# Reordering the first 15 microseconds of a matmul-bound kernel: two normalizations to ScalarE, tiles 0 and 1 by products, weight pieces in half-K groups

## The chip, the cores and the metric

One core of a Trainium2 chip. Kernels are compared only within the same rounds. The time is that of one execution on the device, in microseconds (us). One profiled execution is called "one look", and an execution is called slow here when it took over 621.5 us, a limit that was chosen after the first times were seen.

## The reference

An input x of 2048 rows by 1024 columns is layer-normalized per row. Two branches use the result: a dense layer with a Mish activation (`w1`: 1024x3584, `w2`: 3584x1024) and a diagonal state-space layer (projection by B, a complex scan over 2048 steps, projection by C). Their sum and x make the output.

```python
xn = _layernorm(x, axis=-1)
return x + _A_ref(xn, Lambda, B, C, log_dt, Dskip) + _B_ref(xn, w1, b1, w2)
# _B_ref:  h = xn @ w1 + b1;  act = h * tanh(softplus(h));  return act @ w2
```

## The kernel before

The rows go in four blocks of 512, and a block is four tiles (0 to 3) of 128 rows. Each block runs 28 weight tiles of `w1` (called f), the projection by B, the scan, and the output products. Only the **head**, the first 15 us of block 0, is changed.

To start TensorE before the layer norm is ready, the head multiplies the first seven weight tiles by *raw* x of tiles 0 and 1 (`first_raw`), and corrects mean and scale afterwards on VectorE and GpSimd (`raw_scale`, `raw_add`, with rows spread by `first_spread`). Tiles 2 and 3 are normalized first, transposed on TensorE, and multiplied by the same seven weight tiles (`first_rest`: 56 matmuls of 256 columns, the **milestone** of all that follows). Filler matmuls keep TensorE busy while the first data arrive (from 1.04 us on). Each engine ran its own list in the order of the program (VectorE's statistics of tile 2 start at 8.46 us, after the normalization of 8.00 that stands ahead of them); the helper classes put in the semaphore waits.

```python
# order of emission in the head (cut)
keep_busy(18); first_transpose(0); keep_busy(14); first_transpose(1); keep_busy(6)
for q in range(2):                       # ScalarE: turn tiles 0, 1 out of PSUM, roots
    first_copy(q, AC, 0, 4); first_copy(q, AC, 4, NK)
    first_sums_v(q, 0); first_sums_v(q, 1); first_var_v(q); first_sqrt(q)
first_scale(0); first_apply(0); first_scale(1); first_split(); first_apply(1)   # VectorE
for q in range(2):
    transpose_dma(q)                     # sync queue: DMA transposes of normalized tiles 0, 1
for i in range(4, NRING):
    ring_load()                          # sync queue: weight pieces 5 to 7 (1 to 4 went earlier)
...
for f in range(4): first_raw(f, 0, NK // 2)       # weight piece 1
first_spread()
for f in range(4): first_raw(f, NK // 2, NK)      # weight piece 2
# ... statistics and normalization of tiles 2 and 3 on VectorE ...
first_raw(4, 0, NK // 2); first_raw(5, 0, NK // 2)   # weight piece 3
first_transpose(2); first_copy(2, AC)
first_raw(4, NK // 2, NK); first_raw(5, NK // 2, NK) # weight piece 4
first_transpose(3); first_copy(3, VE)
first_raw(6)
```

`load_x(PO, 1, q)` loads the four x tiles of block 1 from GpSimd's queue after the fourth of eight tables:

```python
for j in range(NJ):
    phases(j)
    if j == 3:
        for q in range(NQ):
            load_x(PO, 1, q)
...
if f in (14, 16, 18, 20): ln_stats_only(1, (f - 14) // 2)   # VectorE
if f < 24 and f % 3 == 2: transpose_B(f // 3)               # sync queue, DMA transposes
```

Of the kernel before, what the change touches and what calls it, by code (L numbers as in the profile page):

```python
# [5 lines left out]
ALU = mybir.AluOpType  # L6
AF = mybir.ActivationFunctionType
DT = mybir.dt

P = 128  # L10
# [146 lines left out]
def build_kernel(nc, A_x, A_Lambda_re, A_Lambda_im, A_B_re, A_B_im, A_C_re, A_C_im,  # L157
                 A_log_dt, A_Dskip, B_w1, B_b1, B_w2, out):
    bf16, f32, i32 = DT.bfloat16, DT.float32, DT.int32
# [6 lines left out]
    NK = D // P  # L166
# [8 lines left out]
    PE = Queue(nc, "pe")  # L175
    VE = Queue(nc, "ve")
    AC = Queue(nc, "ac")
    PO = Queue(nc, "po")
    SP = Queue(nc, "sp")

    def sb(name, shape, dtype):
# [3 lines left out]
    NRING = 7  # L185
# [17 lines left out]
    xnT = sb("xnT", [P, NK, TB], bf16)  # L203
    b_xnT = [Buf("xnT%d" % q, parts=[Buf("xnT%d_%d" % (q, h)) for h in range(2)]) for q in range(NQ)]
# [3 lines left out]
    xx = sb("xx", [P, 2, NQ, D], bf16)  # L208
    b_xx = [[Buf("xx%d_%d" % (i, q), parts=[Buf("xx%d_%d_%d" % (i, q, h)) for h in range(2)])
             for q in range(NQ)] for i in range(2)]  # L210
    s_xx = [[DmaSem(nc, "d_xx%d_%d" % (i, q)) for q in range(NQ)] for i in range(2)]
    xn = sb("xn", [P, NQ, D], bf16)
# [38 lines left out]
    def ps16(i):  # L251
        return ps[:, i, :].bitcast(bf16)
# [28 lines left out]
    def early(name, shape, dtype, where):  # L281
        b_early.append(Buf(name))
        return nc.alloc_sbuf_tensor_at(name, shape, dtype, offset=base_c + where), b_early[-1]
# [6 lines left out]
    rr, b_rr = early("rr", [P, 4], f32, 10240)  # L290
    rh, b_rh = early("rh", [P, 4], bf16, 10272)
    rl, b_rl = early("rl", [P, 4], bf16, 10304)
    ncs, _ = early("ncs", [P, NR], f32, 10752)
    b_ncs = [Buf("ncs%d" % f) for f in range(NR)]
    b_early += b_ncs
    ra = [early("ra%d" % i, [P, 2 * P], f32, 12288 + 1024 * i) for i in range(2)]
    rb = [early("rb%d" % i, [P, 2 * P], f32, 14336 + 1024 * i) for i in range(2)]

# [8 lines left out]
    def load_x(queue, blk, q):  # L307
        r0 = blk * TB + q * P
        i = blk % 2
        queue.dma(lambda e: e.dma_start(xx[:, i, q, :], A_x[0, r0:r0 + P, :]),  # L310
                  s_xx[i][q] if blk else s_x0[q], writes=[b_xx[i][q]])
# [16 lines left out]
    def ring_load():  # L328
        i = n_loaded[0]
        if i >= len(items):  # L330
            return
        n_loaded[0] += 1
        kind, g = items[i]
        s = i % NRING
        if kind == "w1":

            dst = ring[:, s, :].rearrange("p (k f) -> p k f", k=NK // 2)
            r0 = (g % 2) * D // 2
            src = B_w1[r0:r0 + D // 2, (g // 2) * 512:(g // 2 + 1) * 512].rearrange("(k p) f -> p k f", p=P)
        else:  # L340
            dst = ring[:, s, :].rearrange("p (f d) -> p f d", f=2)
            src = B_w2[g * 256:(g + 1) * 256, :].rearrange("(f p) d -> p f d", p=P)
        SP.dma(lambda e: e.dma_start(dst, src), s_ring[s], writes=[b_ring[s]])  # L343

    for i in range(4):
        ring_load()
        if i < 2:
            load_x(SP, 0, 2 + i)


    filler = sb("filler", [P, P], bf16)
# [17 lines left out]
    def first_sums_v(q, h):  # L369
        s = q % 2  # L370
        vop(lambda e: e.bn_stats(stats[:, s, h, :], xx[:, 0, q, h * 512:(h + 1) * 512]),
            reads=[b_xx[0][q].parts[h]], writes=[b_stats[s]])

    def first_var_v(q):
        s = q % 2
        vop(lambda e: e.bn_aggr(mv[:, q, :], stats[:, s, :, :]), reads=[b_stats[s]], writes=[b_mv[q]])

    def first_sqrt(q):
        aop(lambda e: e.activation(rc(q, 1), mv[:, q, 1:2], AF.Sqrt, bias=kon[:, 2:3]),
            reads=[b_mv[q], b_kon], writes=[b_rs1[q]])  # L380

    def first_apply(q):
        vop(lambda e: e.tensor_scalar(xn[:, q, :], xx[:, 0, q, :], mv[:, q, 0:1], root(q),
                                      op0=ALU.subtract, op1=ALU.mult),
            reads=[b_xx[0][q], b_mv[q], b_rr if q < 2 else b_rs1[q]], writes=[b_xn[q]])

    def bank_T(q, k):
        if q < 2 and k >= NK // 2:
            return 4 + q
        return 6 + q % 2  # L390

    def first_transpose(q):

        for k in range(NK):
            bank, d = bank_T(q, k), slice(k * P, (k + 1) * P)
            src, b_src = (xx[:, 0, q, d], b_xx[0][q]) if q < 2 else (xn[:, q, d], b_xn[q])
            PE.mm(lambda e, bank=bank, d=d, src=src: e.transpose(ps16(bank)[:, d], src, ident[:]),  # L397
                  reads=[b_src.parts[k // (NK // 2)], b_ident], writes=[b_ps[bank]],
                  first=k == 0 or bank != bank_T(q, k - 1), last=k == NK - 1 or bank != bank_T(q, k + 1))

    def first_copy(q, queue, k0=0, k1=NK):
        dst, b_dst = (xr, b_xr[q][k0 // 4]) if q < 2 else (xnT, b_xnT[q])
        dst = dst[:, k0:k1, q * P:(q + 1) * P]
        bank = bank_T(q, k0)
        srcp = ps16(bank).rearrange("p (k t) -> p k t", k=NK)[:, k0:k1, :]
        if queue is AC:
            aop(lambda e: e.copy(dst, srcp), reads=[b_ps[bank]], writes=[b_dst])
        else:
            vop(lambda e: e.tensor_copy(dst, srcp), reads=[b_ps[bank]], writes=[b_dst])

    def root(q):
        return rr[:, q:q + 1] if q < 2 else rc(q, 1)

    def first_scale(q):

        y, b_y = root(q), b_rr if q < 2 else b_rs1[q]
        vop(lambda e: e.reciprocal(y, rc(q, 1)), reads=[b_rs1[q]], writes=[b_y])
        if q < 2:
            vop(lambda e: e.tensor_tensor(rr[:, 2 + q:3 + q], mv[:, q, 0:1], y, op=ALU.mult),
                reads=[b_mv[q], b_rr], writes=[b_rr])  # L420

    def first_split():
# [60 lines left out]
    def transpose_dma(q):  # L483
        SP.dma(lambda e: e.dma_start_transpose(xnT[:, :, q * P:(q + 1) * P], xn[:, q, :]),
               s_xnT[q], reads=[b_xn[q]], writes=[b_xnT[q]])
# [3 lines left out]
    def b1(f):  # L489
        return par[:, 3 * NJ + f:3 * NJ + f + 1]  # L490
# [13 lines left out]
    def keep_busy(n, behind=()):  # L504
        for i in range(n):
            PE.mm(lambda e: e.matmul(ps[:, 3, 0:P], lhsT=filler[:], rhs=filler[:], start=True, stop=True),
                  reads=[b_filler] + (list(behind) if i == 0 else []), writes=[b_ps[3]], first=i == 0, last=i == n - 1)

    keep_busy(18)
    first_transpose(0)  # L510
    keep_busy(14)
    first_transpose(1)
    keep_busy(6)
    aop(lambda e: e.activation(rs[:, :, 3], kon[:, 2:3].to_broadcast([P, NQ]), AF.Sqrt), reads=[b_kon], writes=b_rs)
# [5 lines left out]
        first_var_v(q)  # L520
        first_sqrt(q)
    first_scale(0)
    first_apply(0)
    first_scale(1)
    first_split()
    first_apply(1)
    for q in range(2):
        transpose_dma(q)
    for i in range(4, NRING):
        ring_load()  # L530
        if i == 5:
            SP.dma(lambda e: e.dma_start(dsk[:], A_Dskip.partition_broadcast(P)), s_dsk, writes=[b_dsk])

    def w1_tile(base, f, k):

# [4 lines left out]
    def first_raw(f, k0=0, k1=NK):  # L540

        for k in range(k0, k1):
            s, w = w1_tile(0, f, k)
            PE.mm(lambda e, k=k, w=w: e.matmul(ps[:, f, 0:2 * P + 1], lhsT=w, rhs=xr[:, k, 0:2 * P + 1],  # L544
                                               start=k == 0, stop=k == NK - 1),
                  reads=[b_ring[s], b_xr_all, b_xr[0][k // 4], b_xr[1][k // 4]], writes=[b_ps[f]],
                  first=k == 0, last=k == NK - 1)
# [8 lines left out]

    def raw_scale(f):
        (a, b_a), (b, b_b) = ra[f % 2], rb[f % 2]
        vop(lambda e: e.tensor_scalar(ncs[:, f:f + 1], ps[:, f, 2 * P:2 * P + 1], -1.0, None, op0=ALU.mult),
            reads=[b_ps[f]], writes=[b_ncs[f]])  # L560
        vop(lambda e: e.tensor_tensor(a[:], ps[:, f, 0:2 * P], yz[:, 0:2 * P], op=ALU.mult),
            reads=[b_ps[f], b_yz], writes=[b_a])
        pop(lambda e: e.tensor_scalar(b[:], yz[:, 2 * P:4 * P], ncs[:, f:f + 1], b1(f), op0=ALU.mult, op1=ALU.add),
            reads=[b_yz, b_ncs[f], b_par], writes=[b_b])

    def raw_add(f):
        (a, b_a), (b, b_b) = ra[f % 2], rb[f % 2]
# [8 lines left out]

    for f in range(4):
        first_raw(f, 0, NK // 2)
    PE.op(lambda e: e.transpose(ps16(6)[:, 0:NST], st[:, :], ident[0:NST, 0:NST]),
          reads=[b_st, b_ident], writes=[b_ps[6]])  # L580
    aop(lambda e: e.copy(par[:, :], ps16(6)[:, 0:NST]), reads=[b_ps[6]], writes=[b_par])
    first_spread()
    for f in range(4):
        first_raw(f, NK // 2, NK)
    for h in range(2):
        first_sums_v(2, h)
    first_var_v(2)
    first_sqrt(2)
    first_sums_v(3, 0)
    first_scale(2)  # L590
    first_apply(2)
    first_sums_v(3, 1)
    first_var_v(3)
    first_sqrt(3)
    first_raw(4, 0, NK // 2)
    first_raw(5, 0, NK // 2)
    first_transpose(2)
    first_copy(2, AC)
    first_raw(4, NK // 2, NK)
    first_raw(5, NK // 2, NK)  # L600
    raw_scale(0)
    first_scale(3)
    first_apply(3)
    first_transpose(3)
    raw_scale(1)
    first_copy(3, VE)
    first_raw(6)
    raw_add(0)
    for f in range(2, NR):
        raw_scale(f)  # L610
# [366 lines left out]
```

## Time and profile before

| | before |
|---|---|
| time, first three executions | 620.79, 620.87, 623.14 us |
| span of the profiled one | 619.6 us |
| TensorE busy | 616.1 us |
| first raw matmul | 7.01 us |
| milestone: start of the 56 matmuls | 15.45 us |

TensorE is the bound, and the prediction below shows the lines for it. What the change moves between engines are these groups of VectorE's timeline (start, length, line, instruction, result and source, shape, count); the two normalizations at 6.95 and 8.00 stand in the way of the statistics of tile 2 at 8.46.

```profile
6.95 0.55 DVE L383 TENSOR_SCALAR xn<-xx,mv,rr 128x1024 bf16<-128x1024 bf16 x1
...
8.00 0.55 DVE L383 TENSOR_SCALAR xn<-xx,mv,rr 128x1024 bf16<-128x1024 bf16 x1
8.46 1.41 DVE L371 BATCH_NORM_STATS2 stats<-xx 128x6 f32<-128x512 bf16 x2
...
13.00 0.55 DVE L383 TENSOR_SCALAR xn<-xx,mv,rs 128x1024 bf16<-128x1024 bf16 x1
```

### The profile page before, as it was taken

To read this page: it belongs to the slowest core of one execution; us is meant where nothing else is said; L and a number is where in the kernel's file an instruction comes from. 1 tells how busy PE (TensorE), PEld (TensorE's weight loads), DVE (VectorE), ACT (ScalarE), POOL (GpSimd) and SP (SyncE) were. 2 spreads that over 40 slices of the span, in tenths; PEclk is the share of its full clock that TensorE was granted. 3 is DMA by queue.
4 is the path that set the end of the run, shared out by engine and by line. 5 is a ranking of instruction groups with operands and counts; after the bars stand their busy time and mean duration, and the time that the engine had idled before them with its cause. 6 is when DMAs were issued, how large, how long until landed. Compare 5 with 4: busy or idle time off the path is not lost.

```text
span 619.6 us, 7424 instructions
## 1 busy us (share of the span) xinstructions
PE 616.1 (99%) x2957; PEld 288.4 (47%) x2957; DVE 467.3 (75%) x698; ACT 247.5 (40%) x161; POOL 53.1 (9%) x57
## 2 busy tenths in 40 slices
PE   9999999999999999999999999999999999999998
PEld 7644444444444444444444444444444444444444
DVE  6989999999467599998147659999624856999603
ACT  4589997441079940000009992000001999000000
POOL 2899100000100000000010000000000000000000
DMA  8999986840454401783054430286203542033001
GB/s 249 252 254 298 225 167 202 206 136 0 146 191 140 135 2 37 204 201 103 17 187 135 158 114 1 96 184 189 75 35 107 173 162 68 1 123 116 1 0 69
DMA packets 97917, 79.94 MB, mean 129 GB/s; under 512 B 51034, under 2 KB 80346, under 8 KB 97882
## 3 DMA queue, kind: packets, MB, share of 16 engines
q1 hardware_dynamic: 94384, 72.17, 42.3%
q10 hardware_dynamic: 2538, 4.14, 1.8%
q0 software_dynamic: 960, 3.15, 1.8%
q8 instruction: 24, 0.39, 0.3%
q14 instruction: 11, 0.09, 0.1%
HBM read 63.19 MB, written 4.19 MB: 109 GB/s over the span
## 4 chain that ended last, share of the span: by engine, by line
PE 98%; DMA 1%; SPq 1%; issue 0%; DVE 0%
PE ps L820 49%; PE ps L740 29%; PE ps L762 18%; DMA ring<-in_B_w_dram 1%; PE ps L553 1%; PE ps L544 0%; SPq L310 0%; PE ps L834 0%; PE ps L397 0%; SPq L343 0%; SPq L314 0%; DVE xx L888 0%
## 5 line engine op out<-in xcount | busy, mean ns | idle before, releaser
L820 PE MATMUL ps<-ring,act 128*128 128x512 bf16 x896 | 194.0, 379 | 0.0
L740 PE MATMUL ps<-xnT,ring 128*128 128x512 bf16 x840 | 182.0, 379 | 0.0
L718 ACT ACTIVATE act<-hb 128x3584 bf16<-128x3584 bf16 x16 | 50.9, 3183 | 220.6 <-DVE hb L749 220.4
L820 PEld LDWEIGHTS ps<-ring,act 128*128 128x128 bf16 x896 | 87.7, 98 | 105.7
L740 PEld LDWEIGHTS ps<-xnT,ring 128*128 128x128 bf16 x840 | 82.2, 98 | 98.9
L749 DVE TENSOR_SCALAR hb<-ps,par 128x512 bf16<-128x512 f32 (+1 forms) x112 | 80.0, 730 | 52.6 <-PE ps L740 51.7
L762 PE MATMUL ps<-xnT,BT 128*128 128x512 bf16 x512 | 111.2, 379 | 0.0
L820 PE MATMUL ps<-CT,hT 128*128 128x512 bf16 x506 | 109.9, 379 | 0.0
L767 DVE TENSOR_TENSOR mt<-ps,tab 128x1024 bf16<-128x1024 f32 x64 | 75.4, 1219 | 13.3 <-PE ps L762 11.7
L762 PEld LDWEIGHTS ps<-xnT,BT 128*128 128x128 bf16 x512 | 50.1, 98 | 60.4
L820 PEld LDWEIGHTS ps<-CT,hT 128*128 128x128 bf16 x506 | 49.5, 98 | 59.7
L785 DVE TENSOR_TENSOR_SCAN hT<-cs,qi,hT 128x512 bf16<-128x512 f32 x48 | 58.9, 1269 | 0.0
L865 DVE TENSOR_TENSOR xx<-ps,xx 128x1024 bf16<-128x1024 f32 (+1 forms) x16 | 18.8, 1190 | 45.1 <-PE ps L820 45.0
L720 ACT ACTIVATE act<-act 128x3584 bf16<-128x3584 bf16 x16 | 51.0, 3190 | 0.2
L719 ACT ACTIVATE act<-act 128x3584 bf16<-128x3584 bf16 x16 | 51.0, 3190 | 0.2
L790 DVE TENSOR_TENSOR mt<-hT,tab 128x1024 bf16<-128x1024 bf16 x64 | 41.4, 688 | 1.1
L725 DVE TENSOR_TENSOR act<-act,hb 128x3584 bf16<-128x3584 bf16 x16 | 33.2, 2075 | 2.3 <-ACT act L720 2.3
L310 POOL DMA_DIRECT2D xx<-in_A_x_dram x12 | 6.7, 560 | 249.4 <-DVE xx L865 245.1
L694 ACT ACTIVATE ct<-CT,cs 128x512 f32<-128x512 bf16 x16 | 11.5, 718 | 25.3 <-DVE CT L696 25.3
L719 ACT ACT_TABLE_LOAD x16 | 20.5, 1283 | 0.3
L720 ACT ACT_TABLE_LOAD x16 | 20.5, 1283 | 0.3
L785 DVE TENSOR_TENSOR_SCAN hT<-cs,hT 128x512 bf16<-128x512 f32 x16 | 18.7, 1208 | 0.0
(101 smaller groups left out, 294.1 us busy)
## 6 DMA issues: line engine op xcount, KB each, us to landing
ring<-in_B_w_dram SPq DMA_DIRECT2D x112, 512.0 KB, 4.0
out_dram<-xx ACTq DMA_DIRECT2D x15, 256.0 KB, 2.1
xx<-in_A_x_dram POOLq DMA_DIRECT2D x12, 256.0 KB, 4.3
xx<-in_A_x_dram SPq DMA_DIRECT2D x3, 256.0 KB, 4.4
xx<-in_A_x_dram SPq DMA_DIRECT2D x2, 128.0 KB, 2.3
dsk<-in_A_Dskip_dram SPq DMA_DIRECT2D x1, 256.0 KB, 7.4
xnT<-xn SPq DMA_TRANSPOSE x14, 4.6
BT<-in_A_B_re_dram SPq DMA_TRANSPOSE x8, 6.3
```

The costliest lines, as they stand in the source:

```text
L718: aop(lambda e: e.activation(a, hs, AF.Exp), reads=[b_hb[g % 2]], writes=[b_act[g]])
L719: aop(lambda e: e.activation(a, a, AF.Ln, bias=1.0), reads=[b_act[g]], writes=[b_act[g]])
L720: aop(lambda e: e.activation(a, a, AF.Tanh), reads=[b_act[g]], writes=[b_act[g]])
L725: vop(lambda e: e.tensor_tensor(a, a, hs, op=ALU.mult), reads=[b_act[g], b_hb[g % 2]], writes=[b_act[g]])
L740: PE.mm(lambda e, k=k, w=w: e.matmul(ps[:, bank, :], lhsT=w, rhs=xnT[:, k, :], start=k == 0, stop=k == NK - 1), reads=[b_ring[s]] + b_xnT, ...
L749: vop(lambda e: e.tensor_scalar(hb[:, hs, ts], ps[:, bank, ts], b1(f), None, op0=ALU.add), reads=[b_ps[bank], b_par], writes=[b_hbf[hs]])
L762: PE.mm(lambda e, j=j, ci=ci, k=k, bank=bank: e.matmul(ps[:, bank + ci, :], lhsT=BT[:, ci, j, k, :], rhs=xnT[:, k, :], start=k == 0, stop= ...
L767: vop(lambda e, s=s, u=u, j=j: e.tensor_tensor(mt[:, s, :, :], u, tab[:, s, j, :].unsqueeze(1).to_broadcast([P, 2, TB]), op=ALU.mult), rea ...
L785: vop(lambda e, ci=ci, init=init: e.tensor_tensor_scan(out=hT[:, ci, j, :], data0=cj("r", j).to_broadcast([P, TB]), data1=hT[:, ci, j, :], ...
L790: vop(lambda e, s=s: e.tensor_tensor(mt[:, s, :, :], hT[:, :, j, :], tab[:, s, j, :].unsqueeze(1).to_broadcast([P, 2, TB]), op=ALU.mult), ...
L820: PE.mm(lambda e: e.matmul(ps[:, u, :], lhsT=lhsT, rhs=rhs, start=st_, stop=last), reads=reads, writes=[b_ps[u]], first=st_, last=last)
L865: vop(lambda e: e.tensor_tensor(xr, src, xr, op=ALU.add), reads=b_ps[bank:bank + n] + [b_x], writes=[b_x])
```

## The change

The intent: take the two normalizations off VectorE, so that tiles 2 and 3 are ready sooner; issue five weight pieces ahead of the DMA transposes; and arrange the raw matmuls in half-K groups around the transposes of tiles 2 and 3, which now share PSUM bank 7. Tiles 0 and 1 are turned by ordinary products with the identity, whose results are fp32 and take a whole bank per half.

```diff
@@ transfers up front: one more weight piece
         if i < 2:
             load_x(SP, 0, 2 + i)
+    ring_load()
@@ normalization of tiles 0, 1 on ScalarE (bias = -mean * rstd)
     def first_apply(q):
+        if q < 2:
+            aop(lambda e: e.activation(xn[:, q, :], xx[:, 0, q, :], AF.Identity, bias=rr[:, 2 + q:3 + q], scale=root(q)),
+                reads=[b_xx[0][q], b_rr], writes=[b_xn[q]])
+            return
@@ banks, and products in place of transposes
-        if q < 2 and k >= NK // 2:
-            return 4 + q
-        return 6 + q % 2
+        if q < 2:
+            return 4 + q + 2 * (k < NK // 2)
+        return 7
 ...
+            put = (lambda e, bank=bank, o=o, src=src: e.matmul(
+                ps[:, bank, o:o + P], lhsT=src, rhs=ident[:], start=True, stop=True)) if q < 2 else (
+                lambda e, bank=bank, d=d, src=src: e.transpose(ps16(bank)[:, d], src, ident[:]))
@@ order (cut)
-    keep_busy(14)
+    keep_busy(16)
 ...
+    first_apply(1)
+    aop(lambda e: e.copy(par[:, :], ps16(4)[:, 0:NST]), reads=[b_ps[4]], writes=[b_par])
 ...
-    first_raw(4, 0, NK // 2)
-    first_raw(5, 0, NK // 2)
-    first_transpose(2)
-    first_copy(2, AC)
-    first_raw(4, NK // 2, NK)
-    first_raw(5, NK // 2, NK)
+    first_transpose(2)
+    first_copy(2, AC, 0, 4)
+    first_sqrt(3)
+    first_copy(2, AC, 4, NK)
     raw_scale(0)
+    for f in range(4, NR):
+        first_raw(f, 0, NK // 2)
     first_scale(3)
     first_apply(3)
     first_transpose(3)
     raw_scale(1)
     first_copy(3, VE)
-    first_raw(6)
+    for f in range(4, NR):
+        first_raw(f, NK // 2, NK)
+    for q in range(2):
+        transpose_dma(q)
+    for i in range(5, NRING):
+        ring_load()
```

More of the change, by code (lines that the diff above doesn't have):

```diff
@@ L292, in build_kernel @@
     rl, b_rl = early("rl", [P, 4], bf16, 10304)
-    ncs, _ = early("ncs", [P, NR], f32, 10752)
-    b_ncs = [Buf("ncs%d" % f) for f in range(NR)]
-    b_early += b_ncs
+    csum, _ = early("csum", [P, NR], f32, 10752)
+    b_csum = [Buf("csum%d" % f) for f in range(NR)]
+    b_early += b_csum
     ra = [early("ra%d" % i, [P, 2 * P], f32, 12288 + 1024 * i) for i in range(2)]
@@ L382, in first_apply @@
     def first_apply(q):
+        if q < 2:
+            aop(lambda e: e.activation(xn[:, q, :], xx[:, 0, q, :], AF.Identity, bias=rr[:, 2 + q:3 + q], scale=root(q)),
+                reads=[b_xx[0][q], b_rr], writes=[b_xn[q]])
+            return
         vop(lambda e: e.tensor_scalar(xn[:, q, :], xx[:, 0, q, :], mv[:, q, 0:1], root(q),
                                       op0=ALU.subtract, op1=ALU.mult),
-            reads=[b_xx[0][q], b_mv[q], b_rr if q < 2 else b_rs1[q]], writes=[b_xn[q]])
+            reads=[b_xx[0][q], b_mv[q], b_rs1[q]], writes=[b_xn[q]])
     def bank_T(q, k):
-        if q < 2 and k >= NK // 2:
-            return 4 + q
-        return 6 + q % 2
+        if q < 2:
+            return 4 + q + 2 * (k < NK // 2)
+        return 7
     def first_transpose(q):
@@ L396, in first_transpose @@
             src, b_src = (xx[:, 0, q, d], b_xx[0][q]) if q < 2 else (xn[:, q, d], b_xn[q])
-            PE.mm(lambda e, bank=bank, d=d, src=src: e.transpose(ps16(bank)[:, d], src, ident[:]),
-                  reads=[b_src.parts[k // (NK // 2)], b_ident], writes=[b_ps[bank]],
+            o = (k % (NK // 2)) * P
+            put = (lambda e, bank=bank, o=o, src=src: e.matmul(
+                ps[:, bank, o:o + P], lhsT=src, rhs=ident[:], start=True, stop=True)) if q < 2 else (
+                lambda e, bank=bank, d=d, src=src: e.transpose(ps16(bank)[:, d], src, ident[:]))
+            PE.mm(put, reads=[b_src.parts[k // (NK // 2)], b_ident], writes=[b_ps[bank]],
                   first=k == 0 or bank != bank_T(q, k - 1), last=k == NK - 1 or bank != bank_T(q, k + 1))
     def first_copy(q, queue, k0=0, k1=NK):
-        dst, b_dst = (xr, b_xr[q][k0 // 4]) if q < 2 else (xnT, b_xnT[q])
+        dst, b_dst = (xr, b_xr[q][k0 // 4]) if q < 2 else (xnT, b_xnT[q].parts[k0 // 4] if k1 - k0 < NK else b_xnT[q])
         dst = dst[:, k0:k1, q * P:(q + 1) * P]
         bank = bank_T(q, k0)
-        srcp = ps16(bank).rearrange("p (k t) -> p k t", k=NK)[:, k0:k1, :]
+        srcp = (ps[:, bank, :].rearrange("p (k t) -> p k t", k=NK // 2) if q < 2 else
+                ps16(bank).rearrange("p (k t) -> p k t", k=NK)[:, k0:k1, :])
         if queue is AC:
@@ L418, in first_scale @@
         if q < 2:
-            vop(lambda e: e.tensor_tensor(rr[:, 2 + q:3 + q], mv[:, q, 0:1], y, op=ALU.mult),
+            vop(lambda e: e.tensor_scalar(rr[:, 2 + q:3 + q], mv[:, q, 0:1], y, -1.0, op0=ALU.mult, op1=ALU.mult),
                 reads=[b_mv[q], b_rr], writes=[b_rr])
@@ L522, in build_kernel @@
     first_scale(0)
-    first_apply(0)
     first_scale(1)
     first_split()
-    first_apply(1)
-    for q in range(2):
-        transpose_dma(q)
-    for i in range(4, NRING):
-        ring_load()
-        if i == 5:
-            SP.dma(lambda e: e.dma_start(dsk[:], A_Dskip.partition_broadcast(P)), s_dsk, writes=[b_dsk])
+    first_apply(0)
     def w1_tile(base, f, k):
@@ L558, in raw_scale @@
         (a, b_a), (b, b_b) = ra[f % 2], rb[f % 2]
-        vop(lambda e: e.tensor_scalar(ncs[:, f:f + 1], ps[:, f, 2 * P:2 * P + 1], -1.0, None, op0=ALU.mult),
-            reads=[b_ps[f]], writes=[b_ncs[f]])
+        vop(lambda e: e.tensor_scalar(csum[:, f:f + 1], ps[:, f, 2 * P:2 * P + 1], 0.0, None, op0=ALU.add),
+            reads=[b_ps[f]], writes=[b_csum[f]])
         vop(lambda e: e.tensor_tensor(a[:], ps[:, f, 0:2 * P], yz[:, 0:2 * P], op=ALU.mult),
             reads=[b_ps[f], b_yz], writes=[b_a])
-        pop(lambda e: e.tensor_scalar(b[:], yz[:, 2 * P:4 * P], ncs[:, f:f + 1], b1(f), op0=ALU.mult, op1=ALU.add),
-            reads=[b_yz, b_ncs[f], b_par], writes=[b_b])
+        pop(lambda e: e.tensor_scalar(b[:], yz[:, 2 * P:4 * P], csum[:, f:f + 1], b1(f), op0=ALU.mult, op1=ALU.add),
+            reads=[b_yz, b_csum[f], b_par], writes=[b_b])
     def raw_add(f):
@@ L578, in build_kernel @@
         first_raw(f, 0, NK // 2)
-    PE.op(lambda e: e.transpose(ps16(6)[:, 0:NST], st[:, :], ident[0:NST, 0:NST]),
-          reads=[b_st, b_ident], writes=[b_ps[6]])
-    aop(lambda e: e.copy(par[:, :], ps16(6)[:, 0:NST]), reads=[b_ps[6]], writes=[b_par])
     first_spread()
@@ L584, in build_kernel @@
         first_raw(f, NK // 2, NK)
+    PE.op(lambda e: e.transpose(ps16(4)[:, 0:NST], st[:, :], ident[0:NST, 0:NST]),
+          reads=[b_st, b_ident], writes=[b_ps[4]])
     for h in range(2):
@@ L606, in build_kernel @@
     first_copy(3, VE)
-    first_raw(6)
+    for f in range(4, NR):
[4 more added lines that the diff above has]
+        ring_load()
+        if i == 5:
+            SP.dma(lambda e: e.dma_start(dsk[:], A_Dskip.partition_broadcast(P)), s_dsk, writes=[b_dsk])
     raw_add(0)
```

## The prediction

> **What bounds the kernel now.** I read the page first: the share of busy time by engine and the chain that ended last.
>
> ```profile
> PE 616.1 (99%) x2957; PEld 288.4 (47%) x2957; DVE 467.3 (75%) x698; ACT 247.5 (40%) x161; POOL 53.1 (9%) x57
> ...
> PE 98%; DMA 1%; SPq 1%; issue 0%; DVE 0%
> ```
>
> TensorE is busy 616.1 of 619.6 us, and 98% of the chain lies on it. The change can therefore save only TensorE's idle time or remove instructions from it; speed on VectorE or ScalarE is worth nothing in itself. It touches only the code ahead of the second weight stage, so I read the timeline of TensorE alone for the first 22 us (start, length, instruction, count, idle before it and its releaser).
>
> ```profile
> 3.20 1.03 PE L397 MATMUL ps<-ident,xx 128*128 128x128 bf16 x8
> 4.03 1.70 PE L506 MATMUL ps<-filler 128*128 128x128 bf16 x14
> 5.52 1.06 PE L397 MATMUL ps<-ident,xx 128*128 128x128 bf16 x8
> 6.37 0.82 PE L506 MATMUL ps<-filler 128*128 128x128 bf16 x6
> 7.01 1.97 PE L544 MATMUL ps<-xr,ring 128*128 128x257 bf16 x16
> ...
> 9.59 1.96 PE L544 MATMUL ps<-xr,ring 128*128 128x257 bf16 x16
> 11.78 1.07 PE L544 MATMUL ps<-xr,ring 128*128 128x257 bf16 x8 [0.22 <-DMA ring<-in_B_w_dram]
> 12.68 0.61 PE L397 MATMUL ps<-ident,xn 128*128 128x128 bf16 x8
> ...
> 15.45 6.29 PE L553 MATMUL ps<-xnT,ring 128*128 128x256 bf16 x56
> ```
>
> From its first filler at 1.04 us TensorE is hardly ever idle: 0.22 us before 11.78 for the third weight transfer, and about 0.1 us before 9.59, where the second transfer lands (issued 3.21, 6.3 us to landing: 9.51). The list of waits has no TensorE wait at all after 22 us. So **the bound is the matmul stream, and the whole recoverable idle time here is some 0.3 us of 620.9**. The milestone to follow is 15.45 us, the start of the 56 matmuls on tiles 2 and 3: after it the stream is the same in both kernels, so the total should move by what that start moves.
>
> The chain of waits in order of time shows the one thing other than TensorE that sets the head, and the timeline of the DMA queue shows what held it up:
>
> ```profile
> 4.24 7.49 DMA ring<-in_B_w_dram
> 11.73 0.05 issue
> ```
>
> ```profile
> 7.53 5.37 SPq L484 DMA_TRANSPOSE xnT<-xn  x2
> 12.94 1.13 SPq L343 DMA_DIRECT2D ring<-in_B_w_dram  x2
> ```
>
> The third weight transfer takes 7.49 us because the engines are full and two DMA transposes of tiles 0, 1 cut in at 7.53.
>
> [...] 128x1024 COPY in 1.012 us[...], 128x1 sqrt with a bias pointer 0.29 to 0.31 us against 0.21 without. [...] The trace agrees for copies: they run between square roots with no load.
> [...] Here the rate rose (weight loads from 151 to 98 ns) at 6.9 us although 16 transposes lay between 3.2 and 6.3, so this trace does not show harm from them[...].
> [...] In the code the transposes of tile 3 will wait for both copies of tile 2 out of bank 7.
>
> **The change part by part**, all times from the timelines of the kernel before, carried forward by its durations.
>
> *Fillers.* Two more at 107 ns while the clock is low (14 take 4.03 to 5.52): tile 1's products start at 5.73 instead of 5.52. Products cost as transposes did (8 in 0.83 us). The clock rises at 6.9 as before, so the six fillers behind end sooner; raw work starts at about 7.08, +0.07 us.
>
> *VectorE loses two normalizations* (0.55 us each, at 6.95 and 8.00). After the second square root (now 7.68, +0.2, since tile 1's copies start 0.2 later) it does the reciprocal and product until 8.18, then tile 2's statistics (1.41 us) from 8.12 instead of 8.46. The statistics of tile 3 waited for its transfer (10.2); without transposes in the way I take 9.5.
>
> *Transfers.* Five weight transfers go up front and the transposes go behind. The second weight transfer (9.5 before) had only 218 GB/s from 7.1 on, against some 350 around it; without the transposes I take 8.8 for it, 10.7 for the third, 12.1 for the fourth. Both weight waits go: **-0.3 us**.
>
> *ScalarE gains two times 1.22 us.* The first, 8.25 to 9.45, fits ahead of the copy of the scale rows (9.64 to 10.22, 9.70 before). Square root of tile 2: 10.12 to 10.42. The second normalization: 10.35 to 11.55. Copy of parameters: until 11.85.
>
> *Tile 2.* Reciprocal 10.56, normalization on VectorE 10.74 to 11.29. TensorE: raw first halves 7.08 to 8.98, spread to 9.49, second halves (16 at 0.117, with their gaps) to 11.40, parameters 0.1, transposes 11.5 to 11.95. No wait.
>
> *Tile 3.* Its variance is ready at 12.14. The first half-copy of tile 2 takes ScalarE 12.15 to 12.73 just ahead of that square root, which so ends at 12.94 (12.78 before). Reciprocal 13.08, normalization 13.28 to 13.83, against 13.00 to 13.55 before. The second half-copy frees bank 7 at 13.45, so it isn't what ends last. TensorE has twelve first-half matmuls to fill in, 12 x 0.112 = 1.34 us, 11.95 to 13.30. It then **waits 0.58 us for the normalized tile 3**, transposes 13.88 to 14.34, does twelve second halves to 15.68; VectorE's copy of tile 3, 14.55 to 15.24, is in time.
>
> *Sum.* Milestone 15.68 against 15.45: +0.07 (start) - 0.3 (weights) + 0.58 (new wait) is +0.35 by parts, +0.23 by the clock times (the difference is rounding of gaps). The milestone is the better count: 620.87 + 0.23 = 621.1 us. I shade it to **621.0**, because the order of the code was plainly chosen to hide this wait and my chain of ten small steps could be 0.5 us pessimistic.
>
> **Rivals.** *A: the wait for tile 3 does not appear.* If its square root slips in ahead of the half-copy (its variance 0.1 us earlier), tile 3 is ready at 13.3, the wait is gone and the head gains 0.3 us: 620.5. For it: 12.14 and 12.15 are a dead heat. Against: queues are in program order, and the copy is put ahead of the square root. It could only be that the copy starts early too.
> *B: the clock rises earlier.* [...] part of 3.2 to 6.9 runs at the high rate; but raw work still needs the first weights at 6.5 (issued 2.18, 4.3 us) and tile 1's copies, so at most about 0.3 us: 620.6. A later rise in some executions may be what the one run of 623.14 was; the change might alter how often.
> *C: the late transfers starve a later stage.* The DMA queue issues back to back from 12.94 to about 44 us. The fourteenth weight piece is issued at 44.12 and takes 7.3 us (lands 51.4); tile 24 (21.57 + 17 x 1.734 = 51.05) needs it at its fifth matmul, about 51.9. Only half a microsecond to spare, and the fifth-from-last head transfer now leaves about 1 us later. Against: the same bytes are moved by engines already full, so the order changes more than the end. If it binds: +0.5, 621.5.
> *D: ScalarE becomes the bound of the head* if a normalization takes much more than 1.22 us. The first has 0.2 us to spare; at 2 us each everything behind moves by 0.6: 621.7.
>
> **Range and chances.** No branch moves the time by even 0.3%, and 2% would be 12.4 us, which only a new stall in every block could cost. The range is from A and B together with run-to-run spread (620.79 to 623.14 before) at the low end, 620.2, to C or D at the high end, 622.0. Faster by over 2%: 0.005; slower: 0.01; within: 0.985.
>
> **What would show it right or wrong.** In the profile after: no weight-transfer wait of TensorE ahead of 12 us; tile 2's statistics starting near 8.1; ScalarE normalizations of about 1.2 us near 8.25 and 10.35, no extra table load; TensorE idle some 0.6 us at about 13.3 to 13.9, released by VectorE's normalization of tile 3; the 56 matmuls starting near 15.7; no TensorE wait near 52 us. A milestone below 15.3 or a waiting TensorE after 22 us would make it wrong.

What is cut from the text, at the marks, are rules and figures that no trace shows. But the 1.22 us of a normalization on ScalarE, which the clock times use, stood on a formula that is cut. From the measured lines it would be 1.17 to 1.21 us, an estimate: 1.012 us for the copy and twice the 0.08 to 0.10 us that a root with a pointer took longer. That the new normalization needs no table load was the assumption; the trace of before shows loads of 1.28 us at 2.43 and 14.36 us, and none between them, where the first roots and copies run. That products might bring the rise of the rate forward (rival B) was a guess, shown by no trace. Where a text says that the clock rises, the trace shows weight loads of 151 ns until 6.9 us and of 98 to 99 ns right after, at a granted clock of 1.00 throughout. "Engines are full" is a DMA share of 1.06, at 349 GB/s, from 4.24 to 11.73 us.

## The result, and the profile after

The changed kernel took 621.66 us in the median of six executions (620.59 to 623.10), beside 621.46 us of the kernel before (620.79 to 623.14, six executions). The ratio is 0.9998 with a 95% interval of 0.9977 to 1.0018. A ratio here is the mean time of one kernel's fast runs over that of the other's in the same rounds, so it is not quite the ratio of the medians. Five more rounds later gave 621.35 against 620.94 us, ratio 1.0001 (0.9988 to 1.0013).

The page's first part shows that TensorE still fills the span. (VectorE lost two instructions, ScalarE gained three.)

```profile
PE 615.7 (99%) x2959; PEld 288.0 (47%) x2959; DVE 467.0 (75%) x696; ACT 249.8 (40%) x164; POOL 54.5 (9%) x57
```

TensorE's timeline answers to the one in the prediction, in the same columns:

```profile
3.98 1.91 PE L516 MATMUL ps<-filler 128*128 128x128 bf16 x16
5.68 0.71 PE L404 MATMUL ps<-ident,xx 128*128 128x128 bf16 x8
6.23 0.50 PE L516 MATMUL ps<-filler 128*128 128x128 bf16 x6
6.94 1.95 PE L547 MATMUL ps<-xr,ring 128*128 128x257 bf16 x16 [0.21 <-DMA ring<-in_B_w_dram]
...
11.19 0.62 PE L406 MATMUL ps<-ident,xn 128*128 128x128 bf16 x8
11.64 1.50 PE L547 MATMUL ps<-xr,ring 128*128 128x257 bf16 x12
13.46 0.62 PE L406 MATMUL ps<-ident,xn 128*128 128x128 bf16 x8 [0.31 <-DVE xn L388]
13.91 1.51 PE L547 MATMUL ps<-xr,ring 128*128 128x257 bf16 x12
15.26 6.28 PE L556 MATMUL ps<-xnT,ring 128*128 128x256 bf16 x56
```

The weight waits of before (0.22 us ahead of 11.78, and one near 9.59) are gone. In their place stand 0.21 us for the *first* weight piece and 0.31 us for the normalized tile 3. The milestone is at 15.26 instead of 15.45 us, and the span shorter by 0.2 us.

ScalarE's timeline shows who delays tile 3: its square root (12.32) waits behind a half-copy of tile 2 (11.84), and both normalizations take 1.23 to 1.24 us, where the prediction has 1.22.

```profile
8.04 1.24 ACT L385 ACTIVATE xn<-xx,rr 128x1024 bf16<-128x1024 bf16 x1 [0.57 <-DVE rr L429]
...
10.05 1.23 ACT L385 ACTIVATE xn<-xx,rr 128x1024 bf16<-128x1024 bf16 x1
11.29 0.20 ACT L592 CAST par<-ps 128x52 f32<-128x52 bf16 x1
11.84 0.59 ACT L417 COPY xnT<-ps 128x512 bf16<-128x512 bf16 x1 [0.35 <-PE ps L406]
12.32 0.30 ACT L380 ACTIVATE rs<-mv,kon 128x1 f32<-128x1 f32 x1
```

VectorE's timeline shows what moving the two normalizations bought: tile 2's statistics start at 7.84 instead of 8.46. But tile 3 is normalized at 12.85 against 13.00 before, hardly earlier. Of the 0.62 us of lead, 0.53 are left at tile 3's first statistics (9.73 against 10.26, with a wait of 0.24 us for the x tile) and 0.15 at its normalization: most of it goes where the square root stands behind the half-copy, which itself waits for TensorE's transposes of tile 2 at 11.19.

```profile
7.84 1.41 DVE L372 BATCH_NORM_STATS2 stats<-xx 128x6 f32<-128x512 bf16 x2
...
9.73 0.69 DVE L372 BATCH_NORM_STATS2 stats<-xx 128x6 f32<-128x512 bf16 x1 [0.24 <-DMA xx<-in_A_x_dram]
...
12.65 0.16 DVE L427 RECIPROCAL rs<-rs 128x1 f32<-128x1 f32 x1 [0.39 <-ACT rs L380]
12.85 0.55 DVE L388 TENSOR_SCALAR xn<-xx,mv,rs 128x1024 bf16<-128x1024 bf16 x1
```

So in this pair of profiles the change wins 0.2 us. In repeated times nothing of it is seen, and times of either kernel spread over more than 2 us. The experiments ask two things: is the head really better, and what makes the spread?

### The profile page after: what moved, and what is told of

It reads as the page before. It is cut to its first block, busy times and chain, and to the rows that moved or that the text cites. A ratio compares the mean times of both kernels' runs of the same rounds, so it can differ in the third digit from the quotient of the medians.

```text
span 619.4 us, 7430 instructions
## 1 busy us (share of the span) xinstructions
PE 615.7 (99%) x2959; PEld 288.0 (47%) x2959; DVE 467.0 (75%) x696; ACT 249.8 (40%) x164; POOL 54.5 (9%) x57
## 4 chain that ended last, share of the span: by engine, by line
PE 98%; DMA 1%; SPq 0%; DVE 0%; ACT 0%; issue 0%
PE ps L830 49%; PE ps L750 29%; PE ps L772 18%; PE ps L556 1%; PE ps L547 1%; DMA ring<-in_B_w_dram 1%; PE ps L844 0%; PE ps L406 0%; SPq L314 0%; ACT xnT L417 0%; DVE xn L388 0%; PE ps L441 0%; DVE xx L898 0%; SPq L310 0%; ACT rs L380 0%
## 5 line engine op out<-in xcount | busy, mean ns | idle before, releaser
L704 ACT ACTIVATE ct<-CT,cs 128x512 f32<-128x512 bf16 x16 | 11.5, 717 | 25.3 <-DVE CT L706 25.3
```

## The experiments

Theory 1: the total is the milestone plus a constant; the change exchanges weight waits for a wait for tile 3 and for the first weights. Its rival: the small lead came from the matmul rate, which rose at 5.9 us in this profile (weight loads from 147 to 98 ns) and at 6.9 us in that of before (151 to 98 ns). Theory 2, formed after the first looks: what spreads the times lies at 43 to 61 us, outside the head. Its rival: the head makes the spread.

### Both kernels once more

No edit.

> The kernel before, looked at once more, to learn what moves in its head from one execution to the next. Theory 1 (the weight transfers set the head of this kernel): the 56 matmuls on tiles 2 and 3 start within 0.15 us of 15.45 again, wherever between 4 and 7 us the matmul rate rises, and TensorE again waits some 0.2 us for a weight transfer near 11.8. Rival (the rise of the rate sets the head): their start moves by half of what the rise moves.

> The changed kernel once more. Theory 1 (the chain from the first weights to the normalized tile 3 sets the head): start of the 56 matmuls within 0.15 us of 15.26, TensorE idle 0.2 to 0.5 us before the transposes of tile 3. Rival (its 0.19 us lead over the kernel before came from the rate's rise at 5.9 us instead of 6.9): if the rise falls near 6.9 here, the start falls back to about 15.45.

Before: milestone 15.78 (span 619.9 us), with waits of 0.32 and 0.29 us for the second and third weight piece. The miss of the stated 0.15 us is itself the answer: the transfers moved it, not the rate, which rose at about 6.2 here, *earlier* than in the first look. Changed kernel: milestone 15.41 with the same 0.31 us wait for tile 3; the rate rose at about 6.5 (5.9 in the first look) and the first raw matmul came 0.16 us later (7.10), which is what the milestone lost. The first weight piece lay there at 6.8 (issued 2.19, 4.6 us to landing), so in this look the fillers at the low rate (weight loads of 152 ns up to the rise) held up the start: the rival is half right, since a late rise can move the milestone by moving the first raw matmul. But the span was 620.5 us, longer than that of before by 0.6. TensorE's timeline of this look of the changed kernel shows where:

```profile
49.80 2.11 PE L750 MATMUL ps<-xnT,ring 128*128 128x512 bf16 x9
52.76 6.22 PE L750 MATMUL ps<-xnT,ring 128*128 128x512 bf16 x28 [0.86 <-DMA ring<-in_B_w_dram]
```

and its chain of waits (start, length, what) gives the transfer behind that wait:

```profile
42.72 10.00 DMA ring<-in_B_w_dram
52.72 0.05 issue
52.76 6.22 PE ps L750 x28
```

This is the prediction's rival C, a weight piece landing too late for tile 24: 10.0 us from issue to landing, where the same piece took 7.3 and 5.3 in the two looks at the kernel before and 6.8 in the first look at the changed one. It happened in one of the three looks at the unedited changed kernel, so it is not what the change does every time.

### The square root of tile 3 ahead of the half-copies

```diff
-    first_copy(2, AC, 0, 4)
     first_sqrt(3)
+    first_copy(2, AC, 0, 4)
     first_copy(2, AC, 4, NK)
```

> Changed kernel, but the square root of tile 3 stands ahead of both half-copies of tile 2. Theory (the half-copy in front of the root holds up tile 3): root at about 11.95 in place of 12.32, normalized tile 3 at about 13.1 in place of 13.4, the half-copies end at about 13.2; TensorE's wait there shrinks from 0.31 to about 0.1 us and the 56 matmuls start near 15.05. Rival (bank 7 is what ends last): the copies end later than before and the wait stays at 0.3 us, start 15.25.

Normalized tile 3 started at 12.65 instead of 12.85, and the wait moved from VectorE to ScalarE's second half-copy out of bank 7 (0.18 us). So the root's place costs 0.13 us of the 0.31, and the shared bank is next in line. The milestone came 8.19 us after the first raw matmul against 8.32, though at 15.31, since that matmul started late (first weights, 7.12). Both theories were half right.

The span was the longest of all, 621.1 us. VectorE's timeline shows it waiting, in program order, for the first x tile of block 1, and TensorE's shows what that costs 14 us later, since VectorE frees PSUM's banks too late:

```profile
47.33 1.43 DVE L454 BATCH_NORM_STATS2 stats<-xx 128x6 f32<-128x512 bf16 x2 [3.65 <-DMA xx<-in_A_x_dram]
```

```profile
49.67 8.81 PE L750 MATMUL ps<-xnT,ring 128*128 128x512 bf16 x40 [0.46 <-DVE hb L759]
58.31 1.89 PE L772 MATMUL ps<-xnT,BT 128*128 128x512 bf16 x8
61.11 26.07 PE L772 MATMUL ps<-xnT,BT 128*128 128x512 bf16 x120 [0.90 <-DVE hb L759]
```

In the first profile of before that x tile took 4.3 us to land and VectorE waited 1.51 us without harm to TensorE; here it took 6.4 us. Theory 2 comes from this look.

### VectorE normalizes tiles 0 and 1 again

```diff
-            aop(lambda e: e.activation(xn[:, q, :], xx[:, 0, q, :], AF.Identity, bias=rr[:, 2 + q:3 + q], scale=root(q)),
-                reads=[b_xx[0][q], b_rr], writes=[b_xn[q]])
+            vop(lambda e: e.tensor_scalar(xn[:, q, :], xx[:, 0, q, :], mv[:, q, 0:1], root(q),
+                                          op0=ALU.subtract, op1=ALU.mult),
+                reads=[b_xx[0][q], b_mv[q], b_rr], writes=[b_xn[q]])
```

> Changed kernel, but VectorE normalizes tiles 0 and 1 again, in the same places of the order. Theory (moving these two to ScalarE is what brings tiles 2 and 3 forward): two times 0.55 us lie ahead of tile 2's normalization on VectorE, which then ends near 11.9 in place of 11.0; TensorE waits about 0.7 us before the transposes of tile 2; the 56 matmuls start near 15.9. Rival (VectorE has slack): the start stays within 0.2 us of 15.26.

Milestone 16.26, 9.00 us after the first raw matmul against 8.32: moving the normalizations to ScalarE is worth up to 0.68 us *within the new order*, in this one look. VectorE's normalization of tile 2 was delayed less than expected, from 10.52 to 11.58; the transposes of tile 2 waited some 0.2 us, not 0.7, because late weights (a 0.30 us wait for the second piece) had already held TensorE up. The two delays overlap: without the late piece TensorE would have reached those transposes at about 11.5 (an estimate from the changed kernel's 4.25 us after the first raw matmul) and waited for the normalization, which ended at 12.13, all the same. The span, 620.4 us, followed the milestone. So the new order needs ScalarE's help, and the old order, with the raw groups elsewhere, did not.

### Transposes in place of products

```diff
-            put = (lambda e, bank=bank, o=o, src=src: e.matmul(
-                ps[:, bank, o:o + P], lhsT=src, rhs=ident[:], start=True, stop=True)) if q < 2 else (
+            put = (lambda e, bank=bank, o=o, src=src: e.transpose(
+                ps16(bank)[:, o:o + P], src, ident[:])) if q < 2 else (
... (cut: the copies out of PSUM read the bf16 view to match)
```

> Changed kernel, but tiles 0 and 1 are turned by transposes with bf16 results again in place of products. Theory (products are worth nothing here: copies of 512 elements take the same 0.58 us from fp32 and from bf16, and the rise of the rate falls anywhere between 4 and 7 us with either): start of the 56 matmuls between 15.2 and 15.5 as in the changed kernel. Rival[...]: the rate rises later than 7 us and the start moves to 15.6 or later.

Milestone 15.41, 8.32 us after the first raw matmul, to the hundredth as with products. Products are worth nothing in this look. Nor did the rival's signs come: the rate rose at about 6.9 us in this look, and over all fourteen profiles (read from weight loads falling from about 150 to 98 ns) it rose between 3.8 and 7.1 us, 2.8 to 6.1 us after the first filler at 1.04. Both kinds are spread over this: about 3.8, 4.9, 5.0, 5.5, 6.2, 6.9 and 6.9 in the seven looks with transposes, 4.0, 4.1, 5.9, 6.3, 6.5, 7.0 and 7.1 in the seven with products. No run here shows a difference between them, and fillers stood between them in all looks, so this is no test of transposes alone. What sets the moment of the rise is not shown by any trace here.

### The kernel before with all weight pieces ahead of the DMA transposes

```diff
-    for q in range(2):
-        transpose_dma(q)
     for i in range(4, NRING):
         ring_load()
-        if i == 5:
-            SP.dma(lambda e: e.dma_start(dsk[:], A_Dskip.partition_broadcast(P)), s_dsk, writes=[b_dsk])
+    for q in range(2):
+        transpose_dma(q)
+    SP.dma(lambda e: e.dma_start(dsk[:], A_Dskip.partition_broadcast(P)), s_dsk, writes=[b_dsk])
```

> Kernel before, but all seven weight pieces of the head are issued ahead of the two DMA transposes of tiles 0 and 1. Theory (the transposes hold up the second and third weight piece): both waits of TensorE for weights in the head go, and the 56 matmuls start near 15.15 in place of 15.45 to 15.8. Rival (the pieces are limited by the transfer rate alone): the third piece still lands at 11.7 and the start stays.

The look agrees with the theory: the third piece took 6.8 us (landing near 11.0) instead of 7.49 (11.73), both weight waits inside the raw work went, and the milestone was the earliest of all, 14.92. (One of four looks at the old head without this edit, that with the earlier x below, had no such wait either, so one look is not proof; the version with both edits is a second.) TensorE's timeline:

```profile
6.74 1.96 PE L543 MATMUL ps<-xr,ring 128*128 128x257 bf16 x16 [0.29 <-DMA ring<-in_B_w_dram]
8.63 0.19 PE L578 MATMUL ps<-ident,st 52*128 52x52 bf16 x1
...
9.21 2.98 PE L543 MATMUL ps<-xr,ring 128*128 128x257 bf16 x24
12.04 0.61 PE L397 MATMUL ps<-ident,xn 128*128 128x128 bf16 x8
...
14.92 6.29 PE L552 MATMUL ps<-xnT,ring 128*128 128x256 bf16 x56
```

Three lines of transfers do for the old head what the reordering was meant to do: 8.18 us from the first raw matmul to the milestone, against 8.32 of the changed kernel.

### Block 1's x tiles loaded 15 us earlier, in both kernels

```diff
     for j in range(NJ):
         phases(j)
-        if j == 3:
+        if j == 0:
             for q in range(NQ):
                 load_x(PO, 1, q)
```

> Changed kernel, but the loads of the second block's four x tiles leave GpSimd's queue after the first phase table in place of the fourth, some 15 us earlier (near 25 us in place of 41). Theory 2 (what spreads the times by 2 us, and hides the change, is VectorE waiting in order for the first of these tiles at 43 to 47 us, and a weight piece that lands late beside them): no wait of VectorE for x near 45 us, no wait of TensorE after 22 us, all times between 620.4 and 621.4. Rival (the spread comes from the head, from where the matmul rate rises): times still reach 622 to 623.

> Kernel before with the same earlier loads. Theory 2: its times draw together too, 620.7 to 621.6, and lie about 0.2 us (the difference of the heads) above those of the changed kernel with earlier loads. Rival: times still reach 623.

In both profiles VectorE no longer waits for x. The list of its waits between 22 and 85 us (waiting for what: us in total, times, longest) for the kernel before,

```profile
DVE stats L444 <- DMA xx<-in_A_x_dram: 1.5, 1, 1.5
```

and for the same kernel with the edit, where only a wait for TensorE is left:

```profile
DVE mt L767 <- PE ps L762: 2.5, 7, 0.7
```

Kernel before with the edit: 620.25 to 620.65 us, five executions, median 620.47; the kernel before itself in the same rounds: 620.34 to 622.72, median 621.04, four of eleven above 621.5. That is what theory 2 expects, except that the times lie 0.5 us below those of the changed kernel with the edit and not 0.2 above. The changed kernel with the edit: median 620.98, but 621.77 and 622.87 still among six. Here theory 2 failed: another cause of slow executions is left.

The edit removes more than VectorE's wait. The fourteenth weight piece, which leaves the sync queue at 42 to 45 us, took 5.3 to 10.0 us to land in the nine looks with x at its old place, and 5.0 to 6.0 in the five with x moved. So the edit cannot tell whether the late x tile or the late weight piece beside it made the slow executions, and no slow execution of the kernel before was profiled.

### The kernel before with both transfer edits

> Kernel before with both transfer edits: all seven weight pieces ahead of the DMA transposes, and the second block's x loaded some 15 us earlier. Theory 2: the 56 matmuls start near 15.0, the span is that start plus 604.1, no TensorE wait follows, and all times lie between 619.9 and 620.6, the lowest of all versions. Rival (the two edits crowd each other's transfers): the start is 15.3 or later, or times over 621 come back.

Its edit is the two diffs above together. Milestone 15.01, span 619.1 us, no wait afterwards, as expected. The times, 620.36 to 621.33 with median 620.81, are not: two of six lie over 621, which was one of the two signs given for the rival, that the edits crowd each other's transfers (the profile does not show its other sign, a later start). The kernel before had a median of 620.46 in the same rounds (620.15 to 623.79), ratio 0.9999 (0.9977 to 1.0020). The slow executions above 621.5 are gone (none of six against three of eleven), the typical one is not better.

### The changed kernel with earlier x and later DMA transposes of B

```diff
-            if f < 24 and f % 3 == 2:
-                transpose_B(f // 3)
+            if 3 < f and f % 3 == 2:
+                transpose_B(f // 3 - 1)
```

> Changed kernel with the x loads earlier as in x_early_after and, besides, each DMA transpose of the first projection's matrix put off by three weight tiles, so that the weight pieces leave the queue ahead of them. Theory 3 (the slow executions that x_early_after still had come from a weight piece landing late, as the wait of 0.86 us at 52.76 in after_again): all times between 620.2 and 621.2. Rival (they come from the head, from late first weights or x tiles): two of six times still lie above 621.5.

Together with the earlier x: 620.43 to 621.47, median 620.94, none of six above 621.5. This agrees with theory 3 in that no slow one came, though two times (621.40 and 621.47) lie above its stated 621.2. No slow execution of the version without this edit was caught in a profile, so the theory is supported by six times only. In the profiled look the first weights landed late (0.30 us wait, first raw matmul at 7.64), so the head does scatter too, by about 0.9 us.

### The changed kernel timed again, and the earlier x once more

> The changed kernel as it is, timed in five rounds, because 5 of its 7 times so far lie above 621.5 us against 10 of 30 of the kernel before. Theory 2 (the slow executions have the same cause in both and about the same share): one to three of six times above 621.5, median within 0.5 us of the kernel before's. Rival C' (the later weight transfers of the change make the late piece near 52 us more frequent): four or more of six above 621.5, median 621.5 to 621.9 again. Theory 1 for its profile: the 56 matmuls start 8.3 us after the first raw matmul (to 8.9 if the second weight piece is late), and span less that start is 604.1 us plus any later TensorE wait.

> The kernel before with the earlier x loads once more, since its first five times were the tightest of all (620.25 to 620.65). Theory 2 (the late x tile makes the slow executions of this kernel): again no time above 621.5, while the kernel before shows some above 622 in the same rounds. Rival (the first five were luck): about two of six above 621.5.

Changed kernel: 620.70 to 621.89, one of five above 621.5; the kernel before in the same rounds 620.70 to 622.00, three of nine. Rival C' finds no support here, though over all looks the changed kernel stands at six of twelve and the kernel before at 13 of 39; that difference is not resolved. Kernel before with earlier x: 620.54 to 621.04. In its ten executions it never exceeded 621.04; the kernel before was above 621.5 in seven of its twenty executions in the same rounds. The ratios, 0.9986 (0.9973 to 1.0000) and 0.9992 (0.9978 to 1.0005), are still "the same" by any strict reading: the gain is in the slow executions, about 0.1% in the mean.

### The looks side by side

One profile each; times in us. "Between" is the milestone less the first raw matmul, "rest" the span less the milestone.

| kernel | first raw | milestone | between | span | rest |
|---|---|---|---|---|---|
| before | 7.01 | 15.45 | 8.44 | 619.6 | 604.15 |
| before, second look | 6.93 | 15.78 | 8.85 | 619.9 | 604.12 |
| before, x early | 7.08 | 15.21 | 8.13 | 619.3 | 604.09 |
| before, x early, again | 6.79 | 15.60 | 8.81 | 619.7 | 604.10 |
| before, loads first | 6.74 | 14.92 | 8.18 | 619.0 | 604.08 |
| before, both edits | 6.87 | 15.01 | 8.14 | 619.1 | 604.09 |
| changed | 6.94 | 15.26 | 8.32 | 619.4 | 604.14 |
| changed, second look | 7.10 | 15.41 | 8.31 | 620.5 | 605.09 |
| changed, third look | 7.26 | 15.58 | 8.32 | 620.2 | 604.62 |
| transposes | 7.09 | 15.41 | 8.32 | 619.5 | 604.09 |
| root first | 7.12 | 15.31 | 8.19 | 621.1 | 605.79 |
| VectorE normalizes | 7.26 | 16.26 | 9.00 | 620.4 | 604.14 |
| changed, x early | 6.76 | 15.65 | 8.89 | 619.7 | 604.05 |
| changed, x early, B later | 7.64 | 15.97 | 8.33 | 620.1 | 604.13 |

Three readings. First, the rest is 604.05 to 604.15 wherever TensorE has no later wait, so a microsecond of milestone is a microsecond of time. The exceptions are the second look of the changed kernel (0.86 us of it is the wait shown), root first (0.46 + 0.90 of its 1.7 us over), and the third look of the changed kernel, 0.5 us over: there VectorE had waited 3.2 us for the x tile, and the fourteenth weight piece landed at 50.7 us, before its tile needs it at about 52, but some matmul records are missing, so no TensorE wait is listed and its cause is likely rather than shown. Second, where no weight piece is late, "between" is 8.13 to 8.18 in the old order and 8.31 to 8.33 in the new: **the new head is no shorter than the old one, it is merely less exposed to the second and third weight piece** (with its DMA transposes issued early, the old order lost 0.3 to 0.7 us to them in three of four looks; the new one, with ScalarE normalizing, lost 0.6 us in one of seven, when the second piece made it wait 0.36 us). Third, the first raw matmul starts between 6.74 and 7.64, and in nine of the fourteen looks TensorE's wait ahead of it ended with the first weight piece.

## Why the prediction was right or wrong

The time: 621.66 measured in the first six executions against 621.0 stated, inside the range of 620.2 to 622.0, and "within 2%" with near certainty. Yet two thirds of a microsecond is three times the effect that was summed, and the kernel before moved up by as much in the same rounds (621.46): its three first times were too few to know its median. The range holds the unchanged kernel's median as well, so that the time fell into it says nothing for the sum. By the signs that the prediction itself set, it was wrong: the milestone of the first profile, 15.26, lies below 15.3, and TensorE waited after 22 us in the second look.

*What bounds it.* Right. The rest of 604.1 us in eleven looks shows the step that carried the argument, that the total moves by what the milestone moves. The recoverable idle time was put at 0.3 us; the second look at the kernel before had 0.78 (0.17, 0.32 and 0.29), so it was read from one lucky profile.

*Fillers, +0.07 us.* Not to be told from the scatter: the first raw matmul came at 6.94, 7.10 and 7.26, against 7.01 and 6.93 before. Two fillers count for less than when the first weights land (6.87 in the first profile) and when the rate rises.

*VectorE and ScalarE.* Right: 1.23 to 1.24 us for a normalization with 1.22 predicted, no new table load (one at 13.12 us, for one at 14.36 before), tile 2's statistics at 7.84 with 8.12 predicted. (They came early in part because tile 1's products met the higher rate, 0.71 us for eight in place of 1.06; at the low rate, in the second look, they started at 8.00.)

*Transfers, -0.3 us.* Right in the three looks at the changed kernel: no wait for the second or third piece. The same head with the earlier x waited 0.36 us for the second. The figure given for the cause is not in the trace: from 7.1 to 9.5 us the engines of the kernel before moved 345 GB/s, not 218. The second and third piece landed at 9.0 and 11.2 us, later than the 8.8 and 10.7 predicted but in time. A wait for the first piece, unforeseen, took 0.21 and 0.38 us back in two of the three looks.

*Tile 3, +0.58 us.* The mechanism was right, wait and cause as described, and the size wrong: **0.31 us in all three looks.** The chain that ends in it starts on TensorE itself: transposes of tile 2 (11.19), ScalarE's half-copy (11.84) and root (12.32), VectorE's reciprocal (12.65) and normalization (12.85), transposes of tile 3 (13.46). From the first to the last it took 2.27 to 2.28 us in all seven looks in which the root stands behind the half-copy, while the first raw matmul moved from 6.76 to 7.64 us; 2.38 were predicted (11.5 to 13.88). So the wait does not hang on how early the statistics start, and freeing VectorE could not shorten it. The term that was mis-sized by 0.11 us is the step from the root to the reciprocal (13.08, that is 1.58 us after tile 2's transposes, predicted; 1.46 measured). The other 0.16 us lie in TensorE's twelve matmuls in between, put at 1.34 us and shown as busy for 1.50; the profile models their ends, so this part is one of counting.

*Sum.* Milestone 15.68 predicted, 15.26, 15.41 and 15.58 measured; 8.60 us after the first raw matmul predicted, 8.32 measured. Of these 0.28 us, 0.11 is the chain to tile 3 above; the rest lies ahead of the second halves, which start 2.23 us after the first raw matmul and not 2.41. Against the kernel before (15.45 and 15.78) this is a gain of 0.2 us on the average of three and two looks, not a loss of 0.23. But the looks with the earlier x have the same two heads (15.21 and 15.60 before, 15.65 and 15.97 changed), and over all of them the averages are 15.51 for four looks at the old head and 15.57 for five at the new. The sign is therefore not resolved by the milestones; at this size it cannot be seen in the times either.

*Rivals.* A did not happen by itself, and forcing it gained 0.13 us because bank 7 comes next. B is real as scatter (3.8 to 7.1 us), but no look ties it to the products. C was named with the right place and the right transfer, but as a steady effect; it is an occasional one, 0.86 us in one of three looks. D did not happen. What no part of the prediction saw is VectorE waiting in order for block 1's x. Loading it earlier took the slow executions of the kernel before away (none of sixteen), but it sped up the weight piece of C as well, so the share of each stays open.

What stays open: whether the changed kernel has slow executions more often (six of twelve against 13 of 39), and what made the two slow ones that were left with the earlier x.

## What to carry to other kernels

When one engine is busy for 99% of the span, add up its idle time first: it is all that a reordering can win, and here it was less (0.3 and 0.78 us in two looks at the kernel before) than the scatter from one execution to the next (up to 3.6 us). Look at several profiles of the *same* kernel before believing 0.2 us of difference; the rest after a fixed milestone tells at once whether an extra microsecond belongs to the changed part. A load whose consumer sits in an in-order queue should be issued well ahead: with four such loads moved by some 15 us, sixteen timed runs of two versions of the kernel before had no slow execution, while the reordering of the head took away nothing. (In the profiles with the move a weight piece issued at 42 to 45 us landed sooner too; these runs do not separate the two.)
